# Two interleaved read streams for the moving operand of every product, and equal quarters of 480 columns, in an attention and FFN kernel on one core

## The chip, the cores and the metric

The kernel runs on one core of one Trainium2 chip. The metric is the device time of one execution, in microseconds (us); several runs are made, and their median counts. TensorE (PE) multiplies, VectorE (DVE) and ScalarE (ACT) do elementwise work, GpSimd (POOL) and SyncE (SP) mostly issue DMAs. SBUF is the on-chip memory of 128 partitions, PSUM the memory that TensorE writes.

## The reference, cut to what matters

```python
xn = layernorm(x)                                  # x: 1 x 2048 x 640, float32
q, k, v = split(xn @ wqkv)                         # 32 heads of 20 columns
idx = pos[:, None] - 2 * arange(8)[None, :]        # 8 keys, every second position back
attn = softmax(where(idx >= 0, (q . k[idx]) * 20 ** -0.5, -1e9))
s = (attn . v[idx]) @ wo                           # 640 x 640
g = silu(silu(xn @ w1) @ w2)                       # 640 x 1536, 1536 x 640
return x + s * g
```

## The kernel before, in words

The 2048 positions are dealt into four groups of 512 (four tiles of 128, `T = 4`): two halves of the sequence, in each the even and the odd positions, so that a dilated neighbour is a neighbour within a group. Partition p holds neighbouring positions of a group, and the keys and values that a position needs from the partition before come by a small DMA (the halo).

**Products.** Every float32 product is made of three: operand = hi + lo, and hi x hi + lo x hi + hi x lo are added in PSUM. The hi half is a ScalarE copy, the lo half a subtraction. Each of the three is a matmul with a 128 x 128 stationary operand and a moving operand of up to 512 columns, read from SBUF one column after another. There are three kinds:

- Q, K, V (`product` in `first_quarter`, line 910, for the first quarter of the first group; `unit` in `qkv_phase`, lines 972 to 974, for all others): a tile of the activations is stationary, the weights move. A group has four quarters of 8 heads; each quarter has five weight units (640 = 5 x 128 rows), so 5 x 4 tiles x 3 = 60 matmuls. In the first group a quarter has 480 columns (160 of Q, K and V each). In the other groups quarters 0 to 2 have 512: their own 480 and 32 more (`MORE`) of quarter 3's Q; quarter 3 then has 384.
- The first FFN product (`up`, lines 1144 to 1146): a 128 x 128 block of w1 is stationary, 512 positions of the activations move. Its result is transposed, features on partitions; ScalarE applies SiLU twice (lines 1157 and 1158) and VectorE subtracts to get the lo half (line 1159).
- The second FFN product and the output projection (`down`, `wo_phase`, `wo_last`, all through `tm_mm`, lines 1017 and 1019): activations are stationary, a row of 640 weight columns moves in a piece of 384 (`CA`) and one of 256 (`CB`). The last piece of the last tile is line 1130.

**Weights.** Raw weights are loaded from HBM (`raw_load`, issued by SP, the first one by ScalarE's queue), split into hi and lo, and the halves are stored in a DRAM tile; later groups reload them (`w_load`, line 573, issued by GpSimd) into a ring of seven buffers (`RING`). A raw load for Q, K, V in the first group is one DMA of three runs per row; in later groups it has a second DMA for the columns moved between quarters.

**Attention.** After a quarter, ScalarE copies Q, K and V out of PSUM (`evac_qkv`, lines 750, 753, 756), the halo is moved, and VectorE computes the scores and the weighted sums (`scores`, line 793; `values`, lines 827 to 835). The output O of a group is turned by TensorE (lines 645 and 853) or by DMA and is needed by the output projection of that group, which runs in the next group's FFN phase; for the last group it runs at the very end (`wo_last`), with line 853 turning the last pieces inside the last `up`. There VectorE multiplies the gate (line 1098), adds x (line 1100) and SP stores the result (line 1105).

**Order.** The order of TensorE's work is the order in which the program adds it. All other engines' order is planned by a small simulation (`Weave`), with a price for every step; `mm` (line 390) is the price of a matmul of n columns in us. For the first quarter the order is written out by hand (`FIRST`, `ON_VECTOR`, `ON_SCALAR`, `ON_POOL`), and the loads of the input tiles 1 to 3 have priorities (`X_AT = 1.2, 6, 8`) among the raw loads, which have 1 + k.

Of the kernel before, what the change touches and what calls it, by code (L numbers as in the profile page):

```python
# [70 lines left out]
MORE = 32  # L71
# [233 lines left out]
def local_attention_silu_ffn(ctx: ExitStack, tc: tile.TileContext, x, wqkv, wo, w1, w2, out):  # L305
# [84 lines left out]
    mm = lambda n: n / 2400 + 0.0045 + n * 2.1e-5  # L390
# [77 lines left out]
    first_q = NQ * DC  # L468

    def parts(i):  # L470


        _, q, c = units[i]
        cols = [(s * D + q * CQ, CQ) for s in range(3)]
        if i >= first_q:
            if q < NQ - 1:
                cols.append(((NQ - 1) * CQ + q * MORE, MORE))
            else:
                cols[0] = (q * CQ + q * MORE, CQ - q * MORE)
        return cols  # L480
# [9 lines left out]
    def width(i):  # L490
        return sum(n for _, n in parts(i)) if units[i][0] == "q" else D

    def start(i):

        return QAT if i < first_q else 0
# [14 lines left out]
    def raw_load(k):  # L510
# [12 lines left out]
        more = []  # L523
        if u[0] == "q":
            _, q, c = u
            cols, m, at = parts(i), 3, 0
            whole = wqkv[c * P:(c + 1) * P, :]
            src = whole.rearrange("p (s m) -> p s m", s=3)[:, :, q * CQ:(q + 1) * CQ]
            if i >= first_q:
                if q < NQ - 1:  # L530
                    odd, lies = cols[3], 3 * CQ
                else:
                    odd, lies, src, m, at = cols[0], 0, src[:, 1:], 2, cols[0][1]
                more.append((r[:, lies:lies + odd[1]], whole[:, odd[0]:odd[0] + odd[1]]))
            dst = r[:, at:at + m * CQ].rearrange("p (s m) -> p s m", s=m)
        elif u[0] == "w1":
            src = w1.rearrange("(c p) f -> p c f", p=P)[:, :, u[1] * P:(u[1] + 1) * P]
            dst = r.rearrange("p (c f) -> p c f", c=DC)
        else:
            m = wo if u[0] == "wo" else w2  # L540
            src, dst = m[u[1] * P:(u[1] + 1) * P, :], r
# [4 lines left out]
        def go():  # L546
            nc.sync.dma_start(dst, src)
            for to, by in more:
                nc.sync.dma_start(to, by)
        dma(go, [], kr, n * P * 4, 1 + k if k < 2 * DC else clock[0] + 5, (0.62 if k < 2 * DC else 0.45) * (1 + len(more)))  # L550
# [7 lines left out]
    def w_load():  # L558
# [12 lines left out]
        if what[i] == "load":  # L571
            src = halves[u]
            add("POOL", 1.0, lambda: nc.gpsimd.dma_start(both, src), [("half", u), ("half", u, "more")], [kh, kl], due + 10,  # L573
                nbytes=2 * n * P * 4)
            raws_due(i, sum(j < i for j in fresh) - 1)
            return
# [11 lines left out]
        if what[i] == "store":  # L588
            def keep(to, a, b, key):
                dma(lambda: nc.sync.dma_start(to, both[:, :, a:b].bitcast(F32)), [kh, kl], [key], 2 * (b - a) * P * 4,  # L590
                    due + 25)
            wide = width(len(units) - 1 - units[::-1].index(u))
            kept = dram.tile([P, 2, wide], F32, name="half_" + "_".join(map(str, u)))
            halves[u] = kept
            past = n - wide if u[0] == "q" and u[1] == NQ - 1 else 0
            keep(kept[:, :, :n - past], past, n, ("half", u))
            for k in range(past // MORE):
                v = ("q", k, u[2])
                keep(halves[v][:, :, 3 * CQ:], k * MORE, (k + 1) * MORE, ("half", v, "more"))
# [143 lines left out]
    def q_keys(q, t):  # L743
        return [("q", q, t)] + [("q", q, t, k) for k in range(q if q == NQ - 1 else 0)]

    def evac_qkv(g, q, t, ps, kp):
        kv, qq = KV[q], Q[q]
        skip = MORE * q if g and q == NQ - 1 else 0
        n = CQ - skip
        act(2 * CQ, lambda: nc.scalar.activation(  # L750
            kv[:, :, HALO + t, :], ps[:, n:n + 2 * CQ].rearrange("p (s m) -> p s m", s=2), AF.Copy),
            [kp], [(k, q, t) for k in ("kv", "own", "val")], -1 if (g, q) in KEYS_FIRST else 0)
        act(n, lambda: nc.scalar.activation(qq[:, t, skip:], ps[:, :n], AF.Copy), [kp],
            [("q", q, t)] if skip else q_keys(q, t), 0)
        if g and q < NQ - 1:
            act(MORE, lambda: nc.scalar.activation(
                Q[NQ - 1][:, t, q * MORE:(q + 1) * MORE], ps[:, 3 * CQ:], AF.Copy), [kp], [("q", NQ - 1, t, q)], 0)
# [29 lines left out]
    def scores(g, q):  # L787
# [4 lines left out]
        for t in range(0, T, 2):  # L792
            dve(2560, lambda t=t: nc.vector.tensor_tensor(  # L793
                out=PR, in0=win(qq[:, t:t + 2, :], W, 0), in1=win(kv[:, 0, t:t + 2, :], W, CQ), op=OP.mult),
                hk + q_keys(q, t) + q_keys(q, t + 1) + [("own", q, k) for k in range(T)], PRK, pr, lock=True)
# [64 lines left out]
    def first_quarter(i):  # L860
# [41 lines left out]
        def product(t, k, c):  # L902
# [7 lines left out]
            pe(mm(480), lambda: nc.tensor.matmul(  # L910
                o[:, :3 * CQ], x[i][:, c, tsl(t)], w, start=first, stop=last), [(kx, i, c, t), kw], [kp])
# [33 lines left out]
    def qkv_phase(g, i, io):  # L945
# [10 lines left out]
        for q in range(NQ):  # L956
            if g == 0 and q == 0:
                ps = first_quarter(i)
            else:
                turn_now(g, q, io)  # L960
                ps = [bank() for t in range(T)]
                for c in range(DC):
                    wh, wl, kh, kl = w_next("q", q, c)
                    for t in range(T):
# [4 lines left out]
                        def unit(c=c, t=t, o=o, wh=wh, wl=wl, n=n):  # L969
                            o = o[:, :n]  # L970
                            hi, lo = TH[i][:, c, tsl(t)], TL[i][:, c, tsl(t)]
                            nc.tensor.matmul(o, hi, wh, start=c == 0, stop=False)  # L972
                            nc.tensor.matmul(o, lo, wh, start=False, stop=False)  # L973
                            nc.tensor.matmul(o, hi, wl, start=False, stop=c == DC - 1)  # L974
# [37 lines left out]

    def tm_mm(banks, t, st, w, first, last, cols=(0, 1)):
        a, b = banks
        h = t % 2
        if 0 in cols:
            nc.tensor.matmul(a[t][0][:, :CA], st, w[:, :CA], start=first, stop=last)  # L1017
        if 1 in cols:
            nc.tensor.matmul(b[t // 2][0][:, h * CB:(h + 1) * CB], st, w[:, CA:], start=first and h == 0,  # L1019
                             stop=last, skip_group_check=True)  # L1020

    def tm_views(banks):

        a, b = banks
        for k in range(T // 2):
            for t in (2 * k, 2 * k + 1):
                yield a[t][0][:, :CA].rearrange("p (t m) -> p t m", t=1), a[t][1], slice(t, t + 1), slice(0, CA)
            yield b[k][0].rearrange("p (t m) -> p t m", t=2), b[k][1], slice(2 * k, 2 * k + 2), slice(CA, D)
# [4 lines left out]
    TM = mm(CA) + mm(CB)  # L1033

    def wo_phase(g, i):
# [11 lines left out]
        for p, kp, ts, cs in tm_views(banks):  # L1047
            n = (ts.stop - ts.start) * (cs.stop - cs.start)
            dve(n, lambda p=p, ts=ts, cs=cs: nc.vector.tensor_tensor(
                out=G[:, ts, cs], in0=p, in1=G[:, ts, cs], op=OP.mult), [kp], gkeys(ts, cs), 0, late=ADD_LATE)  # L1050
# [28 lines left out]
    def wo_last(g, i):  # L1079
# [9 lines left out]
        kx = lambda t, *cs: [("xin", t, c.start) for c in cs]  # L1089
        for t in range(T):  # L1090
            for cs in ((A,), (B,)) if t < IN_PARTS else ((A, B),):
                at = slice(cs[0].start, cs[-1].stop)
                dma(lambda t=t, at=at: nc.sync.dma_start(xr[t][:, at], rows(xg, g)[:, t, at]), [], kx(t, *cs),
                    P * (at.stop - at.start) * 4, clock[0] - 20)

        def give(p, kp, t, cs):
            n = cs.stop - cs.start
            dve(n, lambda: nc.vector.tensor_tensor(out=G[:, t, cs], in0=p, in1=G[:, t, cs], op=OP.mult),  # L1098
                [kp], [("g", t, cs.start)], 0)
            dve(n, lambda: nc.vector.tensor_tensor(out=xr[t][:, cs], in0=xr[t][:, cs], in1=G[:, t, cs], op=OP.add),  # L1100
                [("g", t, cs.start)], kx(t, cs), 0, lock=True)

        def leave(t, *cs):
            at = slice(cs[0].start, cs[-1].stop)
            dma(lambda: nc.sync.dma_start(rows(og, g)[:, t, at], xr[t][:, at]), kx(t, *cs), [],
# [178 lines left out]
```

## Time and profile before

| | |
|---|---|
| median of 3 runs | 623.72 us (623.28 to 623.80) |
| span of the profiled execution, first to last instruction | 622.2 us |
| median of the runs minus that span | 1.5 us |
| granted TensorE clock | 1.000 |
| TensorE matmul busy | 616.9 us (99%), 3395 instructions |
| weight loads busy | 558.1 us (90%) |
| VectorE busy | 538.1 us (86%) |
| ScalarE busy | 272.1 us (44%) |
| DMA moved | 167.39 MB |

The profile is of one execution, so sums are made against its span of 622.2 us. A line such as `L974` is line 974 of the kernel. In the chain and in the timelines a row has the start, the length (both in us from the span's start), the engine and the line, and `xN` is the number of instructions merged into the row. `PEld` is the loading of a stationary operand, which overlaps matmuls; `SPq` is the issuing of DMAs by SP. In a window's row the busy time of each engine stands behind the stretch, in the order PE, PEld, DVE, ACT, POOL. Matmuls are pipelined: one that lasts 333 ns can start 0.17 us behind the one before it. A group's row gives engine, operation, output <- input with their shapes, count, total busy us and mean ns of one, and the idle time before.

### The profile page before, as it was taken

How to read it: one execution, taken by the hardware profiler on the slowest of the kernel's cores; microseconds unless marked ns; L12 is line 12 of the kernel's file. 1: busy time of each engine (PE TensorE's matmuls, PEld its weight loads, DVE VectorE, ACT ScalarE, POOL GpSimd, SP SyncE). 2: the span in 40 equal slices, each digit the busy share in tenths (PEclk: the TensorE clock that was granted, in tenths of full speed). 3: DMA queues.
4: the chain of work that ended last, by engine and by line, in shares of the span. 5: the costliest groups of instructions: out<-in, count | busy, mean ns of one | idle time of the engine just before them, and what ended most of it. 6: DMA issues, size and time to landing. Idle time of an engine off the chain costs nothing.

```text
span 622.2 us, 9038 instructions
## 1 busy us (share of the span) xinstructions
PE 616.9 (99%) x3395; PEld 558.1 (90%) x3395; DVE 538.1 (86%) x545; ACT 272.1 (44%) x496; POOL 114.5 (18%) x165
## 2 busy tenths in 40 slices
PE   8999999999999999999999999999999999999997
PEld 7888899998889998999888999989988999999997
DVE  6599899999798998998957796799996899999834
ACT  5445556364545324553545612624754273252220
POOL 4800000011110142112221114121222211111100
PEclk9999999999999999999999999999999999999999
DMA  9999999699999999975999999999599999998552
GB/s 295 303 316 309 317 381 367 236 316 271 280 292 311 304 261 321 239 240 141 198 292 268 310 338 364 288 197 248 140 223 282 210 291 294 329 224 301 187 191 86
DMA packets 105114, 167.39 MB, mean 269 GB/s; under 512 B 36605, under 2 KB 66781, under 8 KB 105069
## 3 DMA queue, kind: packets, MB, share of 16 engines
q1 hardware_dynamic: 78573, 87.08, 54.7%
q0 software_dynamic: 25952, 79.31, 45.5%
q8 instruction: 27, 0.44, 0.3%
q10 hardware_dynamic: 544, 0.41, 0.2%
q14 instruction: 18, 0.15, 0.1%
HBM read 107.91 MB, written 34.16 MB: 228 GB/s over the span
## 4 chain that ended last, share of the span: by engine, by line
PE 98%; DMA 1%; DVE 0%; issue 0%
PE acc L1017 22%; PE acc L1019 15%; PE acc L973 10%; PE acc L974 10%; PE acc L972 10%; PE rot L1146 9%; PE rot L1145 9%; PE rot L1144 9%; PE acc L910 2%; PE rot L645 1%; DMA xin<-in_A_x_dram 1%; PE rot L894 0%; PE rot L1130 0%; DVE st L879 0%; PE rot L853 0%; DVE gate L1098 0%
## 5 line engine op out<-in xcount | busy, mean ns | idle before, releaser
L1017 PE MATMUL acc<-w,sh 128*128 128x384 f32 x384 | 113.1, 333 | 0.0
L972 PE MATMUL acc<-w,th 128*128 128x512 f32 (+2 forms) x300 | 112.9, 376 | 0.0
L974 PE MATMUL acc<-w,th 128*128 128x512 f32 (+2 forms) x300 | 112.9, 376 | 0.0
L973 PE MATMUL acc<-w,tl 128*128 128x512 f32 (+2 forms) x300 | 112.9, 376 | 0.0
L1019 PE MATMUL acc<-w,sh 128*128 128x256 f32 x384 | 107.2, 279 | 0.0
L793 DVE TENSOR_TENSOR pr<-q,kv 128x2560 f32<-128x2560 f32 x32 | 90.3, 2821 | 12.5 <-DMA kv<-kv 12.2
L1144 PE MATMUL rot<-th,w 128*128 128x512 f32 x240 | 94.3, 393 | 0.0
L1146 PE MATMUL rot<-th,w 128*128 128x512 f32 x240 | 93.8, 391 | 0.0
L1145 PE MATMUL rot<-tl,w 128*128 128x512 f32 x240 | 93.8, 391 | 0.0
L827 DVE TENSOR_TENSOR pr<-q,kv 128x2560 f32<-128x2560 f32 x32 | 91.8, 2869 | 0.7
L1157 ACT ACTIVATE sh<-rot 128x512 fp32r<-128x512 f32 x48 | 28.7, 598 | 142.5 <-PE rot L1146 142.3
L796 DVE TENSOR_REDUCE l<-pr 128x128 f32<-128x2560 f32 x32 | 90.1, 2814 | 0.3
L573 POOL DMA_DIRECT2D w<-half_q x52 | 37.3, 717 | 234.6 <-PE rot L1146 105.5
L573 POOL DMA_DIRECT2D w<-half_w x72 | 38.4, 534 | 205.1 <-PE acc L1019 84.9
L832 DVE TENSOR_TENSOR pr<-pr 128x1280 f32<-128x1280 f32 x64 | 73.9, 1155 | 1.3
L1019 PEld LDWEIGHTS acc<-w,sh 128*128 128x128 f32 x384 | 72.2, 188 | 0.8
L1017 PEld LDWEIGHTS acc<-w,sh 128*128 128x128 f32 x384 | 72.1, 188 | 0.9
L972 PEld LDWEIGHTS acc<-w,th 128*128 128x128 f32 x300 | 56.3, 188 | 8.8
L973 PEld LDWEIGHTS acc<-w,tl 128*128 128x128 f32 x300 | 56.3, 188 | 8.7
L974 PEld LDWEIGHTS acc<-w,th 128*128 128x128 f32 x300 | 56.3, 188 | 8.7
L1017 PE MATMUL acc<-w,sl 128*128 128x384 f32 x192 | 57.8, 333 | 0.0
L750 ACT ACTIVATE kv<-acc 128x320 f32<-128x320 f32 x64 | 27.4, 440 | 62.2 <-PE acc L974 60.7
(115 smaller groups left out, 1038.4 us busy)
## 6 DMA issues: line engine op xcount, KB each, us to landing
w<-half_w POOLq DMA_DIRECT2D x72, 640.0 KB, 7.3
w<-half_q POOLq DMA_DIRECT2D x39, 512.0 KB, 5.5
half_w<-w SPq DMA_DIRECT2D x24, 640.0 KB
kv<-kv SPq DMA_DIRECT2D x15, 560.0 KB
w<-half_wo POOLq DMA_DIRECT2D x10, 640.0 KB, 10.0
kv<-kv SPq DMA_DIRECT2D x15, 420.0 KB
gate<-in_B_w_dram SPq DMA_DIRECT2D x16, 320.0 KB
w<-half_q POOLq DMA_DIRECT2D x13, 384.0 KB, 6.4
```

The source lines that it names most:

```text
L573: add("POOL", 1.0, lambda: nc.gpsimd.dma_start(both, src), [("half", u), ("half", u, "more")], [kh, kl], due + 10, nbytes=2 * n * P * 4)
L793: dve(2560, lambda t=t: nc.vector.tensor_tensor(out=PR, in0=win(qq[:, t:t + 2, :], W, 0), in1=win(kv[:, 0, t:t + 2, :], W, CQ), op=OP.mult ...
L796: dve(2560, lambda t=t: nc.vector.tensor_reduce(out=l[:, t:t + 2].rearrange("p t w h -> p (t w h)"), in_=PR.rearrange("p t w (h d) -> p (t ...
L827: dve(2560, lambda t=t, v=v: nc.vector.tensor_tensor(out=PR.rearrange("p t w (h d) -> p t (w h) d", d=DH), in0=e[:, t:t + 2].rearrange("p ...
L972: nc.tensor.matmul(o, hi, wh, start=c == 0, stop=False)
L973: nc.tensor.matmul(o, lo, wh, start=False, stop=False)
L974: nc.tensor.matmul(o, hi, wl, start=False, stop=c == DC - 1)
L1017: nc.tensor.matmul(a[t][0][:, :CA], st, w[:, :CA], start=first, stop=last)
L1019: nc.tensor.matmul(b[t // 2][0][:, h * CB:(h + 1) * CB], st, w[:, CA:], start=first and h == 0, stop=last, skip_group_check=True)
L1144: nc.tensor.matmul(h, wh[:, cs], TH[i][:, c, :], start=c == 0, stop=False)
L1145: nc.tensor.matmul(h, wh[:, cs], TL[i][:, c, :], start=False, stop=False)
L1146: nc.tensor.matmul(h, wl[:, cs], TH[i][:, c, :], start=False, stop=c == DC - 1)
```

## The change

All matmuls of the three kinds read their moving operand in two streams: column 0 of the first half, column 0 of the second half, column 1 of the first half, and so on. The access pattern has an outer dimension of n/2 steps of one column and an inner one of two places, `apart` columns from each other. The output in PSUM is written without gaps, so a column pair lies side by side there, and the engines that read PSUM read it in steps of two and put the halves back in order.

For Q, K, V the distance is 240 columns, and the weights are laid out so that the first half holds K and 80 columns of Q, the second V and the other 80; a raw load is therefore two DMAs in every group. For `up` the distance is 256 positions. For the 640-column rows it is 320: the 384 piece takes 192 columns of each half, the 256 piece 128.

Moving 32 columns between quarters (`MORE`) goes: every quarter has 480 columns in every group. The planner's price of a matmul changes too.

```diff
+def two(ap, at, n, apart):
+    a = [list(ap.ap[0]), [1, n // 2], [apart, 2]]
+    return bass.AP(tensor=ap.tensor, offset=ap.offset + at, ap=a)
+def paired(ps, h=2):
+    return ps.rearrange("p (m h) -> p h m", h=h)
+def halves_of(ap):
+    return ap.rearrange("p (h m) -> p h m", h=2)
...
-    mm = lambda n: n / 2400 + 0.0045 + n * 2.1e-5
+    mm = lambda n: n / 2400 + 0.0027
...
     def width(i):
-        return sum(n for _, n in parts(i)) if units[i][0] == "q" else D
+        return 3 * CQ if units[i][0] == "q" else D
...
+            to = halves_of(r)
+            pairs.append((to[:, :, :CQ], whole[:, D:].rearrange("p (s m) -> p s m", s=2)[:, :, q * CQ:(q + 1) * CQ]))
+            pairs.append((to[:, :, CQ:], halves_of(whole[:, q * CQ:(q + 1) * CQ])))
...
+        def go():
+            for to, frm in pairs:
+                by.dma_start(to, frm)
         if k in BY_ACT:
-            add("ACT", 0.65, lambda: nc.scalar.dma_start(dst, src), [], kr, -1, nbytes=n * P * 4)
+            add("ACT", 0.65 * len(pairs), go, [], kr, -1, nbytes=n * P * 4)
             return
...
+        act(2 * CQ, lambda: nc.scalar.activation(kv[:, :, HALO + t, :], paired(ps[:, :2 * CQ]), AF.Copy),
             [kp], [(k, q, t) for k in ("kv", "own", "val")], -1 if (g, q) in KEYS_FIRST else 0)
...
+        act(CQ, lambda: nc.scalar.activation(halves_of(qq[:, t, :]), paired(ps[:, 2 * CQ:3 * CQ]), AF.Copy), [kp], [("q", q, t)], 0)
...
+                            vh, vl = (two(w, 0, n, n // 2) for w in (wh, wl))
+                            nc.tensor.matmul(o, hi, vh, start=c == 0, stop=False)
...
+    def col_a(w):
+        return two(w, 0, CA, D // 2)
+    def col_b(w):
+        return two(w, CA // 2, CB, D // 2)
...
-            nc.tensor.matmul(a[t][0][:, :CA], st, w[:, :CA], start=first, stop=last)
+            nc.tensor.matmul(a[t][0][:, :CA].rearrange("p (m h) -> p m h", h=2), st, col_a(w), start=first, stop=last)
...
-    TM = mm(CA) + mm(CB)
+    TM = mm(CA) + mm(CB) + 0.002
...
-                out=G[:, ts, cs], in0=p, in1=G[:, ts, cs], op=OP.mult), [kp], gkeys(ts, cs), 0, late=ADD_LATE)
+                out=gate(ts, cs), in0=p, in1=gate(ts, cs), op=OP.mult), [kp], gkeys(ts, cs), 0, late=ADD_LATE)
...
+                hi, lo = (two(v[i][:, c, :], 0, TOK, TOK // 2) for v in (TH, TL))
+                nc.tensor.matmul(to, wh[:, cs], hi, start=c == 0, stop=False)
...
-        act(TOK, lambda: nc.scalar.activation(sh, h, AF.Silu), [kp], [("sh", s)], 0, "silu")
+        act(TOK, lambda: nc.scalar.activation(halves_of(sh), paired(h), AF.Silu), [kp], [("sh", s)], 0, "silu")
```

The parts left out treat the other products, drains, input and output pieces of `wo_last` in the same way, with the columns of a piece taken from both halves of a row.

More of the change, by code (lines that the diff above doesn't have):

```diff
@@ L70 @@
 QAT = 48
-MORE = 32
 OAT = 16
@@ L588, in w_load @@
         if what[i] == "store":
[L589 to L593, printed above, removed]
-            halves[u] = kept
[L595 to L599, printed above, removed]
+            kept = dram.tile([P, 2, n], F32, name="half_" + "_".join(map(str, u)))
+            halves[u] = kept
+            dma(lambda: nc.sync.dma_start(kept, both.bitcast(F32)), [kh, kl], [("half", u)], 2 * n * P * 4, due + 25)
         raws_due(i, k)
@@ L1089, in wo_last @@
         kx = lambda t, *cs: [("xin", t, c.start) for c in cs]
+        some = lambda v, at: v if at.stop - at.start == D else of(v, at)
         for t in range(T):
```

99 lines of the change are left out of this document (37 added, 62 removed).

## The prediction

> **What bounds the kernel now.** I read the page first: the busy shares, the granted clock, and the chain that ended last.
>
> ```profile
> span 622.2 us, 9038 instructions
> ...
> PE 616.9 (99%) x3395; PEld 558.1 (90%) x3395; DVE 538.1 (86%) x545; ACT 272.1 (44%) x496; POOL 114.5 (18%) x165
> ...
> PEclk9999999999999999999999999999999999999999
> ...
> PE 98%; DMA 1%; DVE 0%; issue 0%
> ```
>
> TensorE is 98% of the chain, at full clock, and hardly waits. So the time is the sum of its products, and a change acts through what one product costs. Second, the chain by line, which gives the terms of the sum; L910, L972 to L974 are the Q, K, V products, L1144 to L1146 the first FFN products ("up"), L1017 and L1019 the two pieces (384 and 256 columns) of the second FFN product and of the output projection.
>
> ```profile
> by line: PE acc L1017 22.3%; PE acc L1019 15.1%; PE acc L973 10.3%; PE acc L974 10.3%; PE acc L972 10.3%; PE rot L1146 8.8%; PE rot L1145 8.8%; PE rot L1144 8.8%; PE acc L910 2.1%; PE rot L645 0.6%; DMA xin<-in_A_x_dram 0.5%; PE rot L894 0.
> ```
>
> Third, the chain in order of time, for what one product takes. The mean duration that the groups give for a product overlaps the next product, so I use distances from start to start.
>
> ```profile
> 309.79 0.23 PE acc L972
> 310.02 0.23 PE acc L973
> 310.25 0.23 PE acc L974
> 310.47 0.23 PE acc L972
> ...
> 614.34 2.60 PE acc L1017 x15
> 616.93 1.72 PE rot L1130 x15
> ...
> 107.05 0.44 PE rot L645 x4
> ```
>
> 512 columns take 0.227 us (0.68 for three), 384 take 2.60/15 = 0.173, 256 take 1.72/15 = 0.115. The added column from 256 to 384 costs (173.3 - 114.7)/128 = 0.458 ns, while the planner's price list in the kernel counts 1/2400 us = 0.417 ns for one, and all else as an extra. Above n/2400 the products carry 8 ns at 256 columns, 13 at 384, 14 at 512. This extra grows with the columns, at least up to 384, so much of it belongs to the streaming and not to starting a product. A transpose moves only 128 columns and still takes 0.44/4 = 0.11 us: nothing with a weight load of its own has come faster.
>
> **The change: the products.** The count of products stays, and so do the columns: three quarters of 512 and one of 384 make 1920, and so do four of 480. What changes is the order in which the moving operand is read, alternately from two places. No row shows such a read, so its cost is bounded. The change restates the planner's price, from n/2400 + 4.5 ns + n x 0.021 ns to n/2400 + 2.7 ns (a 384+256 pair gets 2 ns more). A price only orders work and proves nothing; but the old list can be tested on the trace. Counts are 576 + 240 = 816 for L1017 (48 second-FFN and 20 output units, 4 tiles, 3 products), 15 fewer for L1019 (those are L1130), 900 for Q, K, V outside the first quarter, 720 for up.
>
> - L1017: 22.3% of 622.2 = 138.8 us, 170 ns each; old list 172.6, new 162.7.
> - L1019: 15.1% = 94.0 us, 117 ns each; old 116.5, new 109.4 + 2.0 = 111.4.
> - Q, K, V: 30.9% = 192.3 us, 213.6 ns each; old 214.6 (mean of its three widths), new 202.7 at 480.
> - Up: 26.4% = 164.3 us, 228.1 ns each; old 228.6, new 216.0.
>
> The old list meets every line within 2%. The lower end of the gain is nothing, or a loss (a rival below); the upper end is the whole extra. All the columns (720 x 512, 540 x 512, 180 x 384, 240 x 480, 816 x 640) are 1,351,680, at n/2400 563 us, against 604 us on these lines with L910 and L1130: 41 us. At 256 columns another end holds: below the 110 ns of a transpose I let no product go, so 7 of the 117 ns can go there, and the new list's 111.4 respects that. I take the new list because it is nearest to the end that the rows set at 256, and because an extra that grows with the columns is what a second read stream could hide. By it, L1017 comes to 816 x 0.1627 = 132.8 (-6.0), L1019 to 801 x 0.1114 = 89.2 (-4.8), Q, K, V to 900 x 0.2027 = 182.4 (-9.9), up to 720 x 0.216 = 155.5 (-8.8), L910 and L1130 together -0.8. Sum **-30.3 us**.
>
> The Trainium skill, "TensorE: Matmul & The Clock Gate", section "Wait — 56ns, not 53.3ns?", states a start-to-start distance of N/2.4 ns plus about 2.5 ns on the warm array, 215.8 at 512 columns. The trace disagrees for today's reading: 227. By that figure (an estimate) the four lines would lose 31.7 instead of 29.5 us and the forecast would be 595.2.
>
> **The head.** In the first group the raw Q, K, V loads become two issues each (K and V, then the two halves of Q). SP issues them one after another, ahead of the input tiles 2 and 3.
>
> ```profile
> 0.75 0.40 SPq L917 DMA_DIRECT2D xin<-in_A_x_dram  x1
> ...
> 1.68 2.68 SPq L547 DMA_DIRECT2D pr<-in_A_wqkv_dram  x4
> ...
> 4.08 0.89 DVE L879 BATCH_NORM_STATS2 st<-xin 128x6 f32<-128x320 f32 x2 [2.63 <-DMA xin<-in_A_x_dram]
> 4.40 0.61 SPq L616 DMA_DIRECT2D xin<-in_A_x_dram  x1
> 5.05 1.40 SPq L547 DMA_DIRECT2D xr<-in_A_wqkv_dram  x2
> 6.49 0.64 SPq L616 DMA_DIRECT2D xin<-in_A_x_dram  x1
> 10.15 0.89 DVE L879 BATCH_NORM_STATS2 st<-xin 128x6 f32<-128x320 f32 x2
> 12.61 0.87 DVE L879 BATCH_NORM_STATS2 st<-xin 128x6 f32<-128x320 f32 x2
> ```
>
> An issue takes 2.68/4 = 0.67 us. Four more put tile 2's issue from 4.40 to 7.1, two more (0.70 each) put tile 3's from 6.49 to 10.6. The first tile was used 3.3 us after its issue (0.75 to 4.08). So tile 2 is there at 10.4 against its use at 10.15, tile 3 at 13.9 against 12.61. That is 0.2 and 1.3 us late, of which other tiles' products cover some. I take **+1.0**, from 0 to +4.1, the whole delay of tile 3's issue. The one load on ACT's queue also doubles, in front of a table load that no product waits for. Later raw loads double too in the first group, while nine small stores go, and the reloads of the split weights keep their bytes. I cost these at nothing; the cover is the ring of seven weight buffers:
>
> ```profile
> w<-half_w POOLq DMA_DIRECT2D x72, 640.0 KB, 7.3
> ```
>
> A reload lands 7.3 us after its issue, and a buffer lasts 15 x 0.227 = 3.4 us, so six buffers give 20 us, 19 at the new pace. Without that cover each issue would cost 0.67 us.
>
> **What is late next: VectorE.** It does the attention and doesn't get faster. The tightest place is the last group.
>
> ```profile
> 175.74 0.49 DVE L835 TENSOR_TENSOR o<-pr 128x320 f32<-128x320 f32 x1
> ...
> 186.01 0.82 PE L645 MATMUL rot<-ident,o 128*128 128x128 f32 x6
> ...
> 449.00:500.00 51.00, 51.00 (x241) 44.01 (x240) 43.44 (x34) 21.37 (x56) 13.20 (x20) 1.00 1.20 224
> 500.00:592.00 92.00, 91.98 (x542) 84.57 (x540) 87.17 (x79) 35.87 (x50) 14.28 (x27) 1.00 1.03 273
> ...
> 471.56 2.82 DVE L793 TENSOR_TENSOR pr<-q,kv 128x2560 f32<-128x2560 f32 x1 [4.70 <-DMA kv<-kv]
> ...
> 590.06 0.49 DVE L835 TENSOR_TENSOR o<-pr 128x320 f32<-128x320 f32 x1
> ...
> 591.83 0.66 PE rot L853 x4
> ```
>
> In the rows of the windows each engine's busy time stands in the order PE, weight loads, VectorE, ScalarE, GpSimd: VectorE is busy 87.17 of the last 92 us. Its scores start at 471.56, after quarter 0 of Q, K, V and the halo transfer, and its last output ends at 590.55, 1.28 us before TensorE transposes it at 591.83. By the prices the group's 240 Q, K, V products fall from 51.5 to 48.6 us (-2.9) and the next 92 us by 30.3/602 of themselves (-4.6): TensorE is there 7.5 us sooner after the group's start, while quarter 0 ends only 60 x (228.6 - 202.7) = 1.6 us sooner. VectorE is then 7.5 - 1.6 - 1.28 = 4.6 us late, less what it can save of its idle 4.8 us in the second window. A part of that idle follows short waits for ScalarE that stay. I take **+3.0**, from 0 to +5 here. The earlier groups have more room (the first group's attention ends at 176.23, and its transposes start at 186.01, 9.8 us later), so I count nothing there, up to +3 if that is gone.
>
> **The drains.** ScalarE and VectorE now read the products from PSUM in steps of two. No row shows that; the nearest have contiguous and strided reads on VectorE.
>
> ```profile
> L804 DVE TENSOR_REDUCE m<-l 128x32 f32<-128x256 f32 x16 | 10.4, 648 | 0.2
> L806 DVE TENSOR_TENSOR l<-l,m 128x256 f32<-128x256 f32 x16 | 6.8, 423 | 0.4
> ...
> L1049 DVE TENSOR_TENSOR gate<-acc,gate 128x384 f32<-128x384 f32 x12 | 6.1, 548 | 0.0
> L1049 DVE TENSOR_TENSOR gate<-acc,gate 128x512 f32<-128x512 f32 x6 | 4.1, 680 | 0.0
> L1157 ACT ACTIVATE sh<-rot 128x512 fp32r<-128x512 f32 x48 | 28.7, 598 | 142.5 <-PE rot L1146 142.3
> ```
>
> L804 reads 256 elements with a large step and takes 1.53 times L806's time. At that rate L1049's 10.2 us grow by 5.4, 1.8 for each of three groups. ScalarE is 44% busy and L1157 waits 142 us for products: covered, and 36 small copies of 32 columns go. At the very end one VectorE multiply lies open, +0.2 at most. I take 0, with +2 inside the range.
>
> **Sum.** 622.2 - 30.3 + 1.0 + 3.0 = 595.9 us for the profiled span. The median of the runs is 623.72, 1.5 above that span, so **597.4 us**.
>
> **The rivals.** (1) *VectorE takes the bound.* The products gain all 30 us, but no VectorE idle is saved (+5), the first hand-over costs +3 and L1049 +2: 622.2 - 30.3 + 1 + 10 + 1.5 = 604.4, with a slow head 607.5. For it: 87.17 of 92 us. Against: it waits elsewhere and the planner may reorder it. Chance 0.13.
>
> (2) *Only some products gain.* The halves lie 240 columns apart for Q, K, V, 256 for up, 320 for the 384/256 pieces; if distance matters, one kind can fail. Without the pieces the gain is 19.4 and TensorE crowds VectorE less: 622.2 - 19.4 + 1 + 1 + 1.5 = 606.3; with the pieces alone (10.8), 614.9. Nothing in the trace tells the kinds apart. Chance 0.07.
>
> (3) *It does not do what it says.* The extra comes from the write side or from the weight loads (90% busy), which stay as they are. Then only the head remains: 624.7. Against: a cost of the loads should not grow with the columns, from 8 to 13 ns. Chance 0.06.
>
> (4) *Slower: switching places at every column.* If each column read from the other place costs an access of its own, every product lengthens. The place is L972 to L974, L1017, L1019 and L1144 to L1146; the price by the nearest strided row, 1.53 times, is 0.53 x 602 = +319, so 943 us. It decides once a 512-column product takes more than today's 0.227 us. For it: VectorE's row. Against: it is another engine. Chance 0.09. The Trainium skill, "SBUF — State Buffer", section "Specifications (TRN2)", says that a 16-byte line needs at least two hits for full bandwidth and that crossing to a new line is penalised; alternating streams cross at every column, so that page speaks for this rival. No run here shows it yet.
>
> **How the numbers follow.** The forecast itself, 590 to 603, has 0.65. A change under 0.2% (1.25 us) can't be told from none. Faster is the forecast with (1) and (2): 0.85; same is (3): 0.06; slower is (4): 0.09. The range goes from 590, where slightly more than the list's gain comes and VectorE keeps up, to 609, which takes in (1) and the first half of (2): 0.62 + 0.13 + 0.04.
>
> **What would show it.** Right: 512-column products 0.216 us apart, 480 at 0.203, pairs at 0.274; TensorE still over 95% of the chain; short TensorE waits for VectorE's output before L853's successor; tile 2 issued near 7 us. Wrong: 512 columns at 0.227 or more; over 8 us of TensorE waits for VectorE; drains of ScalarE and VectorE lengthened by tenths that reach the chain.

## The result and the profile after

The changed kernel takes a median of 640.70 us (639.30 to 643.91, four runs) against 623.76 us of the kernel before (623.28 to 625.18, four runs): a ratio of 1.0275 (95% interval 1.0243 to 1.0307). It is slower by 17 us, where 26 us less had been forecast. (Some executions of e3, e6, e7, e8 and e11 below were over 1.5% longer than the fastest of the same kernel; the ratios leave them out, so a median there need not equal its ratio times the time before.)

First the page of the changed kernel: span, busy time, TensorE's share of each 40th of the span, the granted clock, and the chain by engine.

```profile
span 637.5 us, 9010 instructions
...
PE 598.9 (94%) x3395; PEld 558.6 (88%) x3395; DVE 540.4 (85%) x545; ACT 272.0 (43%) x463; POOL 116.6 (18%) x165
...
PE   8999999996799999999999599999999999997697
...
PEclk9999999999799999999999799999999999999889
...
PE 60%; DMA 15%; DVE 14%; issue 4%; ACT 3%; SPq 3%; POOL 0%; ACTq 0%; DVEq 0%; POOLq 0%
```

TensorE's busy time fell by 616.9 - 598.9 = 18.0 us, but its idle time rose from 622.2 - 616.9 = 5.3 to 637.5 - 598.9 = 38.6 us. The sum, -18.0 + 33.3 = +15.3, is the whole difference of the spans. TensorE has 60% of the chain instead of 98%, and most of the idle time sits in three places: the slices around 160, 360 and 590 us, where the clock also dips.

Did the products get cheaper? The chain in order of time shows the first FFN products (512 columns), a pair of 384 and 256 columns, and Q, K, V (480 columns); read from start to start.

```profile
135.17 0.22 PE rot L1145
135.39 0.22 PE rot L1143
135.60 0.22 PE rot L1144
...
132.34 0.17 PE acc L1008
...
132.62 0.17 PE acc L1008
...
143.99 0.20 PE acc L953
144.19 0.20 PE acc L951
```

512 columns are (135.60 - 135.17)/2 = 0.215 us apart (0.227 before), a pair takes 132.62 - 132.34 = 0.28 (by the distances over longer stretches 0.274; 0.288 before), 480 columns 0.20. These are the values named as the mark of a right forecast. So the loss is in the waits. TensorE's largest ones (us in total, times, longest):

```profile
PE acc L952 <- DVE tl L682: 10.3, 1, 10.3
PE acc L1010 <- ACT kv L732: 7.9, 1, 7.9
PE rot L830 <- DVE o L812: 5.7, 2, 4.3
PE rot L632 <- DVE o L812: 4.7, 1, 4.7
```

Before the change TensorE's longest wait for VectorE was this one, 0.3 us:

```profile
PE rot L894 <- DVE xin L884: 0.3, 1, 0.3
```

The longest wait of the changed kernel can be read on VectorE itself. `tl` is the lo half of the activations for the next Q, K, V products (line 695 before, 682 after); it takes 0.69 us. VectorE's timeline of the kernel before:

```profile
150.29 2.82 DVE L827 TENSOR_TENSOR pr<-q,kv 128x2560 f32<-128x2560 f32 x1
153.03 0.68 DVE L695 TENSOR_TENSOR tl<-turn,th 128x512 fp32r<-128x512 f32 x1
153.63 2.35 DVE L832 TENSOR_TENSOR pr<-pr 128x1280 f32<-128x1280 f32 x2
```

and ScalarE's and VectorE's of the changed kernel (L804 is the multiplication L827, `th` the hi half that `tl` is subtracted from):

```profile
150.21 0.63 ACT L681 ACTIVATE th<-turn 128x512 fp32r<-128x512 f32 x1
...
149.76 2.82 DVE L804 TENSOR_TENSOR pr<-q,kv 128x2560 f32<-128x2560 f32 x1
...
163.06 0.69 DVE L682 TENSOR_TENSOR tl<-turn,th 128x512 fp32r<-128x512 f32 x1
```

Before, the lo half was put in between two steps of the attention. Now both of its inputs are ready at 150.84 (150.21 + 0.63), and it still stands behind 13 us of attention and one weight split (149.76 to 163.06) in VectorE's written-out order; TensorE stands still for it. The 7.9 us wait is of the same kind: ScalarE's timeline of the changed kernel has two weight splits in front of the emptying of PSUM, and they wait for a raw load of the output projection's weights.

```profile
357.85 0.74 ACT L577 ACTIVATE w<-xr 128x640 fp32r<-128x640 f32 x1 [2.02 <-DMA xr<-in_A_wo_dram]
358.95 0.74 ACT L577 ACTIVATE w<-xr 128x640 fp32r<-128x640 f32 x1 [0.37 <-DMA xr<-in_A_wo_dram]
359.60 1.40 ACT L732 ACTIVATE kv<-acc 128x320 f32<-128x320 f32 x4
```

Before, the emptying (L750) came first and the splits (L582) behind it:

```profile
349.75 0.76 ACT L750 ACTIVATE kv<-acc 128x320 f32<-128x320 f32 x2
...
350.48 1.39 ACT L582 ACTIVATE w<-xr 128x640 fp32r<-128x640 f32 x2
```

A wait also slows what follows it. The chain after the first and the second of these waits:

```profile
163.80 0.77 PE acc L952
164.57 0.40 PE acc L953
...
167.21 0.20 PE acc L951
...
360.72 0.58 PE acc L1010
...
364.50 0.32 PE acc L1008
...
365.03 0.16 PE acc L1008
```

Products run at half rate until 167.2 and 365.0, that is 3.4 us from the first restart (163.80) and 4.3 us from the second (360.72). The granted clock in the profile says the same: around the first wait it is 1.00 from 153.5 to 156.5, 0.50 from 157.2 to 163.8, 0.54 from 163.8 to 167.2 and 1.00 behind that; around the second it is 0.97 from 352.8 to 358.4, 0.51 from 360.7 to 365.0 and 1.00 behind that. The Trainium skill, "TensorE: Matmul & The Clock Gate", section "What's actually happening", has the clock fall to half after an idle window of about 3.4 us and come back after a busy one; the trace agrees, though the clock fell some 3.5 us into the first wait and some 5.5 us into the second. Half rate for 3.4 and 4.3 us puts off 1.7 and 2.2 us of work (an estimate from these stretches), so each of the two waits costs some 2 us more than its own length. It is also a reason why TensorE's busy time fell by only 18.0 us here, where the same reading without such waits (e6 below) saves 29.7.

### The profile page after: what moved, and what is told of

It reads as the page before. It is cut to its first block, busy times and chain, and to the rows that moved or that the text cites. A ratio compares the mean times of both kernels' runs of the same rounds, so it can differ in the third digit from the quotient of the medians.

```text
span 637.5 us, 9010 instructions
## 1 busy us (share of the span) xinstructions
PE 598.9 (94%) x3395; PEld 558.6 (88%) x3395; DVE 540.4 (85%) x545; ACT 272.0 (43%) x463; POOL 116.6 (18%) x165
## 4 chain that ended last, share of the span: by engine, by line
PE 60%; DMA 15%; DVE 14%; issue 4%; ACT 3%; SPq 3%; POOL 0%; ACTq 0%; DVEq 0%; POOLq 0%
PE acc L1008 16%; PE acc L1010 10%; DMA kv<-kv 7%; PE rot L1143 6%; PE rot L1145 6%; PE rot L1144 6%; PE acc L952 5%; PE acc L951 5%; PE acc L953 5%; DVE pr L809 3%; DVE pr L804 3%; DMA xin<-xin 2%; DVE l L773 2%; DMA gate<-in_B_w_dram 2%; DVE pr L770 2%
## 5 line engine op out<-in xcount | busy, mean ns | idle before, releaser
L952 PE MATMUL acc<-w,tl 128*128 128x480 f32 x300 | 110.8, 369 | 10.3 <-DVE tl L682 10.3
L951 PE MATMUL acc<-w,th 128*128 128x480 f32 x300 | 111.0, 370 | 1.8 <-ACT q L734 1.3
L953 PE MATMUL acc<-w,th 128*128 128x480 f32 x300 | 110.6, 369 | 0.4 <-POOL w L581 0.4
L1008 PE MATMUL acc<-w,sh 128*128 128x384 f32 x384 | 109.0, 329 | 0.0
L1010 PE MATMUL acc<-w,sh 128*128 128x256 f32 x384 | 104.9, 273 | 0.0
L804 DVE TENSOR_TENSOR pr<-q,kv 128x2560 f32<-128x2560 f32 x32 | 90.3, 2823 | 0.8
L1010 PEld LDWEIGHTS acc<-w,sh 128*128 128x128 f32 x384 | 73.9, 193 | 0.6
L1008 PEld LDWEIGHTS acc<-w,sh 128*128 128x128 f32 x384 | 73.0, 190 | 0.8 <-DVE w L581 0.2
L951 PEld LDWEIGHTS acc<-w,th 128*128 128x128 f32 x300 | 57.2, 191 | 7.4 <-ACT q L734 2.1
L953 PEld LDWEIGHTS acc<-w,th 128*128 128x128 f32 x300 | 57.3, 191 | 4.8 <-POOL w L581 0.8
L1008 PE MATMUL acc<-w,sl 128*128 128x384 f32 x192 | 55.9, 329 | 0.0
L1143 PEld LDWEIGHTS rot<-th,w 128*128 128x128 f32 x240 | 46.6, 194 | 8.7 <-ACT sf L1157 1.8
```

What stands on the lines that cost most here:

```text
L804: dve(2560, lambda t=t, v=v: nc.vector.tensor_tensor(out=PR.rearrange("p t w (h d) -> p t (w h) d", d=DH), in0=e[:, t:t + 2].rearrange("p ...
L951: nc.tensor.matmul(o, hi, vh, start=c == 0, stop=False)
L952: nc.tensor.matmul(o, lo, vh, start=False, stop=False)
L953: nc.tensor.matmul(o, hi, vl, start=False, stop=c == DC - 1)
L1008: nc.tensor.matmul(a[t][0][:, :CA].rearrange("p (m h) -> p m h", h=2), st, col_a(w), start=first, stop=last)
L1010: nc.tensor.matmul(b[t // 2][0][:, h * CB:(h + 1) * CB].rearrange("p (m h) -> p m h", h=2), st, col_b(w), start=first and h == 0, stop=las ...
```

## The experiments

Theories at the start: **A**, the new price gives the planner an order with waits; **B**, the layout (equal quarters, two issues per raw load) collides on SP's queue; **C**, VectorE cannot follow the faster products. From the second set on there was also **D**: the order that the planner writes out holds waits as soon as anything moves its prices or steps, and the order of before is one point without them; and **E**, the added issues themselves cost. D came from the planner's own list, read out: for the changed kernel it already leaves TensorE idle at the three places where the chip shows the waits, for the kernel before nowhere. The planner's list is not a time of the chip, so D had to be run. How an order comes to be without waits stands in the kernel: `plan` looks through its own list for stretches in which TensorE would idle and tries, up to `TRIES = 90` times, to remove them by putting one step of another engine ahead of another. For the kernel before nothing is left; for the changed kernel 34 us are left (the expectation of e6).

**e1, the changed kernel with the old price.**

```diff
-    mm = lambda n: n / 2400 + 0.0027
+    mm = lambda n: n / 2400 + 0.0045 + n * 2.1e-5
-    TM = mm(CA) + mm(CB) + 0.002
+    TM = mm(CA) + mm(CB)
```

> The changed kernel with one part undone: the planner's price of a product is that of before (n/2400 + 4.5 ns + n x 0.021 ns, no 2 ns for a pair). Theory A (the new price makes an order of the other engines that does not hold): the waits go, 595 to 605 us. Theory B (480 columns in every quarter put the halo copies, the DMA transposes and the raw loads in each other's way on SP's queue): still 630 to 645 us. Theory C (VectorE cannot follow faster products, in whatever order): still 630 to 645 us. In all three the products stay 0.203 us apart at 480 and 0.216 at 512 columns.

Measured: 644.55 us, ratio 1.0320 (1.0280 to 1.0359). The old price doesn't bring the time back, so A alone is not the cause. Yet the changed kernel's waits for `tl` and `kv` are gone and others stand in their place, the largest in four parts:

```profile
PE rot L1143 <- ACT sf L1157: 12.3, 4, 4.7
```

So the layout is enough for waits of its own.

**e2, the two halves read one after the other**, with the new price and layout. The columns of K, V and Q land in other places.

```diff
-    a = [list(ap.ap[0]), [1, n // 2], [apart, 2]]
+    a = [list(ap.ap[0]), [apart, 2], [1, n // 2]]
```

> The changed kernel with the reading undone: the moving operand is read half after half, PSUM is drained accordingly; the layout of 480 columns and the new price stay. The products should be 0.215 us apart at 480 and 0.227 at 512 columns again, some 30 us more in all. Theory A: the order planned for faster products waits less on slow ones, but not less than before: 624 to 645 us. Theory B: the collisions stay, 640 to 665 us. Theory C: slow products leave VectorE its room, 622 to 627 us.

Measured: 659.95 us, 1.0580 (1.0556 to 1.0604). Against the changed kernel's 640.70 this is 19 us: what the alternating read is worth inside this order. The chain shows 512 columns and pairs at the old distances, so two pieces as such bring nothing; the alternation does.

```profile
299.90 0.23 PE rot L1143
300.12 0.23 PE rot L1144
300.35 0.23 PE rot L1145
```

**e3, both undone**: e2's edit and e1's together, which leaves the layout and the two issues (columns of K, V and Q land in other places again).

> Only the layout of 480 columns with its two issues for each raw load: reading half after half, price as before. Theory A and theory C: 622 to 627 us, as before. Theory B: the collisions are there without the streams, over 635 us.

Measured: 653.05 us, 1.0443 (1.0394 to 1.0492). With the halves read one after the other and the old price, the layout alone costs over 4%. Whether it is the issues (B) or another order (D), this run can't say.

**e5, the kernel before with the streams and the new price**, in the layout of before.

```diff
-    mm = lambda n: n / 2400 + 0.0045 + n * 2.1e-5
+    mm = lambda n: n / 2400 + 0.0027
-                            o = o[:, :n]
+                            o = duo(o[:, :n])
+                            vh, vl = (two(w, 0, n, n // 2) for w in (wh, wl))
...
-                            nc.tensor.matmul(o, hi, wh, start=c == 0, stop=False)
+                            nc.tensor.matmul(o, hi, vh, start=c == 0, stop=False)
...
-    TM = mm(CA) + mm(CB)
+    TM = mm(CA) + mm(CB) + 0.002
```

> The kernel before with the two streams in all products and the new price alone: quarters of 512, 512, 512 and 384 columns, one issue for a raw load of the first group, and PSUM drained without steps, so that columns of the result are exchanged. Theory A: the new price still makes a bad order, 625 to 645 us. Theory B: the collisions are gone, 592 to 603 us. Theory C: VectorE cannot follow, 615 to 645 us. The products should be 0.216 us apart at 512 columns.

Measured: 632.44 us, 1.0139 (1.0102 to 1.0177), slower than before without any of the layout. B is not the whole cause. Its two largest waits are the changed kernel's, at the same steps:

```profile
PE acc L984 <- DVE tl L705: 11.3, 1, 11.3
PE acc L1030 <- ACT kv L760: 9.2, 1, 9.2
```

**e6, as e5 with the price of before**, so with the order of before: the streams alone.

```diff
-    mm = lambda n: n / 2400 + 0.0027
+    mm = lambda n: n / 2400 + 0.0045 + n * 2.1e-5
```

> The kernel before with the two streams in all products and nothing else: quarters, issues, price and so the program's order are those of before; PSUM is drained without steps, so that columns of the result are exchanged. Theory C (VectorE cannot follow faster products in any order): 615 to 635 us, with TensorE waiting for VectorE in all groups. Theory D (the planner writes an order with waits in it as soon as layout or price move; the plan of the changed kernel has 34 us of TensorE waits in it, that of before none): the order of before has no such waits, so 597 to 610 us, with short waits near the end.

Measured: ratio 0.9641 (0.9569 to 0.9713); median 608.50 of four executions between 598.19 and 614.04; the profiled one is the fastest. In its trace every engine carries out the same instructions in the same order as before, with nothing changed but the operands of the products. Its page and its largest wait:

```profile
span 596.4 us, 9038 instructions
...
PE 587.2 (98%) x3395; PEld 546.6 (92%) x3395; DVE 535.7 (90%) x545; ACT 270.6 (45%) x496; POOL 115.3 (19%) x165
...
PE acc L1028 <- DVE sl L1171: 1.9, 1, 1.9
```

TensorE is busy 29.7 us less (616.9 - 587.2) and idle 9.2 us, 3.9 more than before. VectorE, 90% busy, keeps up. C falls. Between e5 and e6 stands nothing but the planner's price: 1.0139/0.9641 = 1.052.

**e4, the kernel before with nothing but the new price** (the first and the last pair of lines of e5's diff).

> The kernel before with the new price alone: same reading, same quarters. The products take 0.227 us at 512 columns as before. Theory C: nothing to follow, 622 to 627 us. Theory D: the order planned for faster products (28 us of waits in its plan, at three places near 150, 349 and 582 us) waits at the same places: 630 to 650 us.

Measured: 654.42 us, 1.0499 (1.0454 to 1.0545), above even D's 650. TensorE has the same products in the same order as before, VectorE its 545 instructions and GpSimd its 165; ScalarE has one table load more (497 instructions against 496). What differs is the order on VectorE, ScalarE, GpSimd and of the DMA issues, and it costs 31 us. In rows: one stretch of this kernel, then the same stretch of the kernel before, and e4's waits (behind the stretch stand PE, PEld, DVE, ACT, POOL; then clock, DMA share, GB/s).

```profile
140.00:175.00 35.00, 24.66 (x113) 20.69 (x113) 29.67 (x29) 17.05 (x33) 3.57 (x5) 0.85 0.89 223
```

```profile
140.00:175.00 35.00, 35.00 (x170) 29.85 (x169) 31.27 (x30) 18.70 (x43) 4.99 (x7) 1.00 1.14 272
```

```profile
PE acc L973 <- DVE tl L695: 10.3, 1, 10.3
PE rot L853 <- DVE o L835: 6.2, 2, 3.3
PE acc L1019 <- ACT kv L750: 4.2, 1, 4.2
```

The steps waited for are those of the changed kernel's three places (`tl`, `kv`, `o`), in a kernel whose products, loads and layout are those of before.

**e13, the kernel before with its price 1% lower.** Is the new price a bad one, or is any other price?

```diff
-    mm = lambda n: n / 2400 + 0.0045 + n * 2.1e-5
+    mm = lambda n: 0.99 * (n / 2400 + 0.0045 + n * 2.1e-5)
```

> The kernel before with one number changed: the planner's price of a product times 0.99. Reading, layout, issues, and so all work on the chip, are those of before; only the order of the engines other than TensorE can move. Theory D: the plan of before is one point at which no waits are left; at 0.99 the plan has 19 us of waits in it, so 632 to 650 us. Theory C or E (the work itself costs, not its order): 622 to 627 us.

Measured: 649.97 us, 1.0440 (1.0391 to 1.0490). One per cent in the price moves the time by 4.4%. Its largest wait is at a new place, a weight reload, the second at one known from e4:

```profile
PE acc L1017 <- DMA w<-half_w: 6.8, 1, 6.8
PE rot L853 <- DVE o L835: 4.1, 1, 4.1
```

So it is not that the new price is too low for products that got cheaper (in e13 they did not): the order of before is a point without waits, and the one tried beside it has them. That is D. (Its order also makes ScalarE load four tables more: 500 instructions against 496.)

**e7, the kernel before with 480 columns in every quarter**, one issue per raw load, old price.

```diff
-        if i >= first_q:
+        if False:
...
-        return QAT if i < first_q else 0
+        return QAT if units[i][0] == "q" else 0
...
-        return [("q", q, t)] + [("q", q, t, k) for k in range(q if q == NQ - 1 else 0)]
+        return [("q", q, t)]
```

> The kernel before with 480 columns in every quarter of every group, one issue for each raw load of Q, K, V in all groups; reading and price as before. Theory C: 622 to 627 us. Theory D: its plan has 6.5 us of waits and ends 6.4 us later than that of before, so 629 to 640 us.

Measured: 631.06 us, 1.0102 (1.0079 to 1.0125), within what D expected.

**e8, the kernel before with two issues** for each Q, K, V raw load of the first group, and the planner told of both.

```diff
+            if m == 3 and not more:
+                more.append((r[:, at:at + CQ], whole[:, q * CQ:(q + 1) * CQ]))
+                dst, src = dst[:, 1:], src[:, 1:]
...
-            add("ACT", 0.65, lambda: nc.scalar.dma_start(dst, src), [], kr, -1, nbytes=n * P * 4)
+            add("ACT", 0.65 * (1 + len(more)), both_of, [], kr, -1, nbytes=n * P * 4)
```

> The kernel before with two issues (K and V, then Q) for each raw load of Q, K, V of the first group, and nothing else. By the prediction's term for the head: 623.8 + 1, from 0 to +4. Theory D: its plan has 4.9 us of waits and ends 4.8 us later, so 627 to 636 us, and most of it not in the head.

Measured: 648.59 us, 1.0257 (1.0206 to 1.0309). That is far above D's 627 to 636, and it scatters (637.98 to 666.40): the planner's list names waits, but not how long they will be on the chip. Is it the issues, or the order that follows from them?

**e10, as e8, but the planner is told of one issue**, which leaves the order of before.

```diff
-            add("ACT", 0.65 * (1 + len(more)), both_of, [], kr, -1, nbytes=n * P * 4)
+            add("ACT", 0.65, both_of, [], kr, -1, nbytes=n * P * 4)
...
-        dma(go, [], kr, n * P * 4, 1 + k if k < 2 * DC else clock[0] + 5, (0.62 if k < 2 * DC else 0.45) * (1 + len(more)))
+        dma(go, [], kr, n * P * 4, 1 + k if k < 2 * DC else clock[0] + 5, (0.62 if k < 2 * DC else 0.45) * (1 + (len(more) if i >= first_q else 0)))
```

> As the run with two issues for each raw load of Q, K, V in the first group, but the planner is told of one issue, so that the program's order is that of before on every engine and only 20 more issues stand in it. Theory D (the order is what costs): the loss of that run, 14 to 29 us, shrinks to the issues themselves, 624 to 629 us. Theory E (the issues themselves cost: each is 0.67 us on SP's queue, and what is queued behind it is late): still 635 to 655 us.

Measured: 630.24 us, 1.0105 (1.0089 to 1.0122). Its span and its largest wait:

```profile
span 626.4 us, 9072 instructions
...
PE acc L917 <- DVE tl L906: 2.3, 1, 2.3
```

In the trace every engine's order is that of before, with 20 issues more. The issues themselves cost 1.05%, some 6 us, a little over D's 624 to 629 (E has that much of it); the order that follows from telling the planner of them costs about as much again and more: 1.0257 against 1.0105. The wait at L917 is in the first quarter, the head. The lo half that it waits for stands on VectorE behind a step of the layer norm, which waits for an input tile that SP issued at 16.87 us, 12.66 before:

```profile
22.96 0.50 DVE L630 BATCH_NORM_STATS2 st<-xin 128x6 f32<-128x320 f32 x1 [3.98 <-DMA xin<-in_A_x_dram]
```

**e11, the changed kernel, with the planner told the old price and one issue.** The try to give the whole change a good order.

```diff
-    mm = lambda n: n / 2400 + 0.0027
+    mm = lambda n: n / 2400 + 0.0045 + n * 2.1e-5
...
-            add("ACT", 0.65 * len(pairs), go, [], kr, -1, nbytes=n * P * 4)
+            add("ACT", 0.65, go, [], kr, -1, nbytes=n * P * 4)
```

> The changed kernel with its streams, its layout and its two issues, but the planner is given the price of a product of before and the price of one issue for a raw load of the first group; only the equal quarters move its plan, which then has 10 us of waits at two places near 161 and 185 us. Theory D: between the streams in the old order (608) and the changed kernel (641), 610 to 630 us. Theory E: the issues cost as before, 635 to 650 us.

Measured: 650.92, 645.66, 649.65 and 632.02 us, too far apart for a ratio, and all above the 610 to 630 that theory D expected: a miss. The equal quarters still shift the planner's steps, and its own list still has idle stretches of TensorE, so this was no order of before. It says nothing for D, and whether some order lets this layout run near 600 us stays open.

**e12, the streams with every column in its place, in the layout, issues, price and order of before.** It is e6 with the halves of a product next to each other, and the drains reading PSUM in steps of two. K then lies in both halves, so ScalarE empties K in two steps and V in one; the planner isn't told of the added ScalarE copies.

```diff
+        def keys():
+            for s, a, b, lies in ((0, n, mid, 0), (0, mid, n + CQ, mid - n), (1, n + CQ, n + 2 * CQ, 0)):
+                nc.scalar.activation(kv[:, s, HALO + t, lies:lies + b - a], every(ps, total, a, b), AF.Copy)
...
-            nc.tensor.matmul(duo(a[t][0][:, :CA]), st, two(w, 0, CA, D // 2), start=first, stop=last)
+            nc.tensor.matmul(duo(a[t][0][:, :CA]), st, two(w, 0, CA, CA // 2), start=first, stop=last)
...
-        act(TOK, lambda: nc.scalar.activation(sh, h, AF.Silu), [kp], [("sh", s)], 0, "silu")
+        act(TOK, lambda: nc.scalar.activation(halves_of(sh), paired(h), AF.Silu), [kp], [("sh", s)], 0, "silu")
```

> The streams on the kernel before with every column in its place: quarters of 512 and 384 columns, one issue, price and order of before; halves of each piece are paired, PSUM is drained in steps of two, and K is copied in two parts, V in one (128 small ScalarE copies more, of which the planner is not told). Theory D: the order holds, 597 to 612 us, faster than both kernels. Theory C, or stepped drains that cost more than a tenth each: over 615 us.

Measured: 604.42 us (603.24 to 605.58), 0.9687 (0.9667 to 0.9706): 19 us less than before, 36 less than the changed kernel, with the same reading of the operand.

```profile
span 603.8 us, 9166 instructions
...
PE 589.7 (98%) x3395; PEld 546.3 (90%) x3395; DVE 538.5 (89%) x545; ACT 276.8 (46%) x624; POOL 114.3 (19%) x165
```

In one table, the parts against the kernel before, by the ratio alone:

| price | layout, issues | plain read | two streams |
|---|---|---|---|
| old | as before | 1 | 0.9641 (e6), 0.9687 (e12) |
| new | as before | 1.0499 (e4) | 1.0139 (e5) |
| old | changed | 1.0443 (e3) | 1.0320 (e1) |
| new | changed | 1.0580 (e2) | 1.0275 (the change) |

The streams make each row faster, by 1.2 to 3.6%. Every row but the first carries an order other than that of before, and with the plain read these rows cost 4.4 to 5.8%. In the two rows with the changed layout that includes the added issues themselves, some 1% by e10. The costs don't add up: with the old layout the price costs 5%, with the changed one, where the order is bad already, nothing to 1.3%.

## Why the prediction was wrong, point by point

**"A price only orders work and proves nothing"** is the step that failed. It was used to test the price list, and then the order itself was costed at nothing: no term of the sum, no rival and no end of the range stood for another order of ScalarE, VectorE and the queues; rival 1 even counts "the planner may reorder it" as a help. e4 prices it: +31 us with the new price alone, and its waits are for the changed kernel's steps. e13 shows that it needs no large step, and e3 that the changed layout costs 4.4% even at the old price, of which the issues are some 1%. The planner's list of the changed kernel, with its 34 us of waits, could have been read before the forecast. The prediction held the profile of before for the profile of a kernel of this kind; it was the profile of one order, 98% TensorE because in that order the lo halves and the drains came in time.

**The products, -30.3 us.** Right. Without a change of order TensorE's busy time falls by 29.7 us (e6), 27.2 in e12. The distances are those of the new list. The list itself was chosen, not derived from a row, so that the size came out so well is partly luck. The Trainium skill's figure ("TensorE: Matmul & The Clock Gate", section "Wait — 56ns, not 53.3ns?"), N/2.4 + about 2.5 ns, from which 512 columns come to 215.8 ns (an estimate), had disagreed with the plain read's 227; the alternating read's 215 to 216 agrees with it.

**Column counts neutral.** Right for TensorE's work; but equal quarters are another list of steps, and e7 has them at +1.0%.

**The head, +1.0.** Right in place, and near in size, for the delay that was worked out (0.2 us for tile 2, 1.3 for tile 3). VectorE's first steps on tiles 2 and 3 in the changed kernel, against 10.15 and 12.61 before:

```profile
10.90 0.89 DVE L856 BATCH_NORM_STATS2 st<-xin 128x6 f32<-128x320 f32 x2 [0.70 <-DMA xin<-in_A_x_dram]
...
13.71 0.89 DVE L856 BATCH_NORM_STATS2 st<-xin 128x6 f32<-128x320 f32 x2 [0.32 <-DMA xin<-in_A_x_dram]
```

They are 0.75 and 1.1 us late. But the later raw loads, "costed at nothing", belong to it too: two issues in the order of before cost 626.4 - 622.2 = 4.2 us between the two profiled spans (e10; 6 by the ratio), of which the wait at L917, for an input tile issued behind later raw loads, is 2.3. The price given for a lost cover, 0.67 us an issue, was not added anywhere.

**VectorE in the last group, +3.0, and 0 before it.** The mechanism is real, its size belongs to the order. In e6 TensorE shows no wait over 0.2 us for an output of the attention: the term is near zero there. In the changed kernel TensorE waits 5.7 us at L830 and 4.7 at L632 for such outputs. "Over 8 us of TensorE waits for VectorE" had been named as what would prove the forecast wrong: 10.3 + 5.7 + 4.7 = 20.7. They were there, but not by rival 1's mechanism, since VectorE is 85% busy in the changed kernel and 90% in e6: it had the time, and used it on other steps first.

**The drains, 0.** Right. The changed kernel's groups beside L1157 (598) and L1049 (548) of before:

```profile
L1156 ACT ACTIVATE sh<-rot 128x512 fp32r<-128x512 f32 x48 | 28.7, 598 | 142.9 <-PE rot L1145 142.9
...
L1043 DVE TENSOR_TENSOR gate<-acc,gate 128x384 f32<-128x384 f32 x12 | 6.2, 550 | 0.0
```

**The rivals.** (4), slower by switching places at every column, gave the right sign for a wrong reason: alternating reads are the faster ones. The Trainium skill, "SBUF — State Buffer", section "Specifications (TRN2)", would have a column read alone out of its 16-byte line pay a penalty; for TensorE's moving operand, read 240 to 320 columns apart, the trace disagrees, 0.215 against 0.227 us. (2) and (3) fall with the distances. None of the four was the one that happened.

That the sum's 595.9 us is nearly e6's span of 596.4 is no proof of its parts, and in part luck, since that span is the fastest of four executions: the head's +1.0 is not in e6, and VectorE's +3.0 is not there either; short waits and gaps of 3.9 us stand in their place.

What stays open: why the alternating read is faster (the runs show only that it is the alternation and not the splitting), and whether the changed layout has an order without waits.

## What to carry to other kernels

Where a kernel's order is computed from prices, a change of a price or of the list of steps is a change of the order of every engine, and needs a term in the sum: here 1% (e7) to 5% (e4) against a gain of 3 to 4%. Measure a new way of doing a product in the old order first (e6), then let the planner move, and read the waits that its own list already shows before a run. And in the profile of a full engine look at what is placed in front of the short steps that feed it: here a 0.7 us subtraction behind 13 us of other work held TensorE up for 10.3 us.

## What the runs showed of the hardware

- A float32 moving operand that is read alternately from two places, 240 to 320 columns apart (128 to 256 in e12), takes less time than one read straight through: 0.215 against 0.227 us at 512 columns, 0.274 against 0.288 for the 384 and 256 pair. Reading the two halves one after the other (e2) takes the old time.
- ScalarE and VectorE read PSUM in steps of two at the price of a contiguous read (598 ns and 598 for 512 columns on ScalarE; 550 and 548 for 384 on VectorE).
- After waits of 10.3 and 7.9 us TensorE ran at half rate for 3.4 and 4.3 us (granted clock 0.54 and 0.51, 1.00 behind that).
